# Mask, scores and probabilities times V in 64x64 quarters of TensorE's array

## The chip, the cores and the metric

One core of a Trainium2 chip runs one program. Its engines are TensorE (PE; its weight loads are listed apart as PEld), VectorE (DVE), ScalarE (ACT), GpSimd (POOL) and SyncE (SP), which issues most DMAs. The metric is the device time of one execution in microseconds, as the median of several runs. The profile comes from one execution; its span runs from the first to the last instruction.

## The reference

Block-sparse attention (4 batches, 8 heads, 768 tokens, head size 64) is followed by a mixture of experts with top-1 cosine routing (3072 tokens of width 512, 8 experts, hidden width 1024). All inputs are float32.

```python
scores = scale * np.matmul(q, k.transpose(0, 1, 3, 2))      # scale = 1/8
mask = np.abs(blk_i - blk_j) <= 1                           # blocks of 32 tokens
mask = mask | (blk_i == 0) | (blk_j == 0) | (blk_i == n_blocks - 1) | (blk_j == n_blocks - 1)
for qb in range(n_blocks):
    for kb in sampled_blocks[qb]:                           # 3 random blocks of each
        mask[qb * block:(qb + 1) * block, kb * block:(kb + 1) * block] = True
scores = np.where(mask, scores, -1000000000.0)
attn = np.exp(scores - np.max(scores, axis=-1, keepdims=True))
attn = attn / (np.sum(attn, axis=-1, keepdims=True) + 1e-09)
out = np.matmul(attn, v)                                    # then (B,H,S,D) -> (B*S, H*D) = x
# router: logits = normalised x @ normalised expert_emb.T / tau; the best expert of each token
# out[token] = gate * (relu(x @ w1[e]) @ w2[e])
```

## The kernel before

**Stages.** The program builds the mask (lines 83 to 128), runs the attention with the routing of each batch in between (`attention_fast`, line 521), sorts the tokens by expert (`dispatch`) and computes 19 expert tiles of 256 tokens (`fetch`, `expert_tile`). A second, exact attention stands behind a branch that is not taken here.

**Attention.** Two heads form a pair; there are 16 pairs, 4 for each batch. A unit is one chunk of 128 keys against one half (384) of the queries, for both heads of a pair: 6 units go through the keys for one half of the queries (a group of six), 12 make a pair, 192 the whole. Scores lie with keys on the partitions and queries on the free axis, so that the exponentials are at once the moving operand of the product with V. Key and query vectors are turned so that head 0 has partitions 0 to 63 and head 1 has 64 to 127.

The parts of a unit, by name and line:

- *Mask* (L272, in `score_fast`): for each head one bfloat16 matmul over 24 block rows writes 0 or about -1e9 into the score's PSUM bank. `kmask` and `qmask` hold the 24 rows twice, from partition 0 and from partition 32.
- *Scores* (L275): for each head one float32 matmul, 64 rows to 128 keys, 384 queries wide, is added to it. Each head has its own PSUM bank.
- *Exponential* (L278): ScalarE, 768 columns, from PSUM into the tile e (4 buffers). No maximum is taken off.
- *Sum over keys* (L291, L293): VectorE adds up e for the denominators in esum.
- *AV* (L295, in `attend_fast`): for each head one float32 matmul, 128 keys to 64 output rows. Head 0 writes partitions 0 to 63 and head 1 64 to 127 of one PSUM bank, added up over 6 units; this accumulator has 2 buffers. After the sixth, ScalarE copies it into the tile at (L299).
- *Settle* (L313 to L323), once for six units: 3 transposes of at, 12 records of one-column matmuls that sum esum over partitions, and three operations on VectorE that divide and write x.
- *Turn* (L257 to L261), four for each pair: 3 transposes of the next pair's keys or queries; VectorE copies the keys, ScalarE scales the queries.
- *Route* (from L348), once for each batch: transposes of x, logits, choice of expert, ranks.

**PSUM.** Eight banks: two score buffers of two banks (`big`, which route's transposes also use), two of one bank for AV (`acc`), two of one bank for turns and settle (`small`).

**Order.** In iteration u the code issues the loads of the pair after next (at the head of a pair), the scores of unit u+1, a turn (at units 2, 4, 8 and 10 of a pair), AV of unit u, and at the second unit of each six the settle of the six before, with route at the end of a batch. The framework's planner places instructions on each engine by their priority in the code and by its own estimate of when their buffers and inputs are free, so what waits can be passed by what follows. Each engine works through its own queue; semaphores tie the queues together.

```python
if u + 1 < units:
    score_fast(n, u + 1)
if u % per in (2, 4, 8, 10) and g + 1 < pairs:
    turn_fast(n, g + 1, (2, 4, 8, 10).index(u % per))
attend_fast(n, u)
if u % NC == 1 and u > NC:
    settle(n, u // NC - 1)
```

Of the kernel before, what the change touches and what calls it, by code (L numbers as in the profile page):

```python
# [10 lines left out]
F32 = mybir.dt.float32  # L11
# [3 lines left out]
ALU = mybir.AluOpType  # L15
AX = mybir.AxisListType
PSUM = bass.MemoryType.PSUM

P = 128
B, H, S, D = 4, 8, 768, 64  # L20
BLK = 32
NB = S // BLK
NRAND = 3
NC = S // P
# [11 lines left out]
HALF = S // 2  # L36
# [9 lines left out]
def iota(k, name, shape, pattern, base=0, mult=0):  # L46
    t = k.const.tile(shape, F32, name=name)
    k.nc.gpsimd.iota(t, pattern=pattern, base=base, channel_multiplier=mult,
                     allow_small_or_imprecise_dtypes=True)
    return t  # L50
# [32 lines left out]
def build_mask(k):  # L83


    nc, pool = k.nc, k.setup
    ids = pool.tile([NB, NRAND], I32, name="ids")
    words = dataclasses.replace(k.blocks.tensor, shape=[NB, 2 * NRAND], dtype=I32)
    with nc.allow_non_contiguous_dma(reason="low words of the block numbers"):
        nc.sync.dma_start(out=ids, in_=bass.AP(tensor=words, offset=0, ap=[[2 * NRAND, NB], [2, NRAND]]))  # L90
    ids_f = pool.tile([NB, NRAND], F32, name="ids_f")
    nc.vector.tensor_copy(out=ids_f, in_=ids)

    dif = iota(k, "dif", [NB, NB], [[1, NB]], mult=-1)
    col = iota(k, "col", [NB, NB], [[1, NB]])
    row = iota(k, "row", [NB, NB], [[0, NB]], mult=1)
    m = pool.tile([NB, NB], F32, name="m")
    nc.vector.tensor_tensor(out=m, in0=dif, in1=dif, op=ALU.mult)
    nc.vector.tensor_scalar(out=m, in0=m, scalar1=1.5, scalar2=None, op0=ALU.is_le)
    for val in (0.0, float(NB - 1)):  # L100
        for pos in (col, row):
            nc.vector.scalar_tensor_tensor(out=m, in0=pos, scalar=val, in1=m, op0=ALU.is_equal, op1=ALU.max)
    for r in range(NRAND):
        nc.vector.scalar_tensor_tensor(out=m, in0=col, scalar=ids_f[:, r:r + 1], in1=m,
                                       op0=ALU.is_equal, op1=ALU.max)
    nc.vector.tensor_scalar(out=m, in0=m, scalar1=1.0, scalar2=-NEG, op0=ALU.subtract, op1=ALU.mult)

    oh = pool.tile([P, NC, NB], F32, name="oh_blk")
    nc.gpsimd.memset(oh, 1.0)
    nc.gpsimd.affine_select(out=oh, in_=oh, pattern=[[1, NC], [-BLK, NB]], compare_op=ALU.is_ge,  # L110
                            fill=0.0, base=0, channel_multiplier=NC)
    nc.gpsimd.affine_select(out=oh, in_=oh, pattern=[[-1, NC], [BLK, NB]], compare_op=ALU.is_ge,
                            fill=0.0, base=BLK - 1, channel_multiplier=-NC)
    kr = k.big.tile([P, 1024], F32, name="kr", tag="big")
    for c in range(NC):
        nc.tensor.transpose(kr[0:NB, c * P:(c + 1) * P], oh[:, c, :], k.ident)
    krow = pool.tile([NB, S], F32, name="krow")
    nc.vector.tensor_copy(out=krow, in_=kr[0:NB, 0:S])
    qr = k.big.tile([P, 1024], F32, name="qr", tag="big")
    for lo, hi in ((0, 512), (512, S)):  # L120
        nc.tensor.matmul(qr[0:NB, lo:hi], lhsT=m, rhs=krow[:, lo:hi], start=True, stop=True)

    if not k.exact:
        k.kmask = k.const.tile([P, S], BF16, name="kmask")
        k.qmask = k.const.tile([P, S], BF16, name="qmask")
        for h in range(2):
            nc.vector.tensor_copy(out=k.kmask[32 * h:32 * h + NB, :], in_=krow)
            nc.scalar.copy(out=k.qmask[32 * h:32 * h + NB, :], in_=qr[0:NB, 0:S])
        return
    k.sides = []  # L130
    for i in range(2):
        side = {}
        for name, rows, copy in (("q", qr[0:NB, 0:S], nc.scalar.copy), ("k", krow, nc.vector.tensor_copy)):
            for h in range(2):
                side[name, h] = k.const_x.tile([D + NB, S], F32, name=f"{name}{h}_{i}")
                copy(out=side[name, h][D:D + NB, :], in_=rows)
        k.sides.append(side)
# [110 lines left out]
def turn_fast(k, g, part):  # L248

    nc = k.nc  # L250
    name, lo = ("k", "q")[part // 2], part % 2 * NQ
    if part == 0:
        k.turned[g] = {n: k.tp.tile([P, S], F32, name=f"{n}t", tag=f"{n}t") for n in ("k", "q")}
    src, dst = k.loaded[g]["kq".index(name)], k.turned[g][name]
    ps = k.small.tile([P, 512], F32, name="turn", tag="small")
    for c in range(NQ):
        nc.tensor.transpose(ps[:, c * P:(c + 1) * P], src[:, lo + c].rearrange("p h d -> p (h d)"), k.ident)  # L257
    if name == "q":
        nc.scalar.mul(out=dst[:, lo * P:lo * P + HALF], in_=ps[:, 0:HALF], mul=SCALE)
    else:  # L260
        nc.vector.tensor_copy(out=dst[:, lo * P:lo * P + HALF], in_=ps[:, 0:HALF])  # L261


def score_fast(k, u):

    nc = k.nc
    g, qh, kc = u // (2 * NC), u // NC % 2, u % NC
    kt, qt = k.turned[g]["k"], k.turned[g]["q"]
    ps = k.big.tile([P, 2, 512], F32, name="sc", tag="big")
    keys, queries = slice(kc * P, (kc + 1) * P), slice(qh * HALF, (qh + 1) * HALF)  # L270
    for h in range(2):
        nc.tensor.matmul(ps[:, h, 0:HALF], lhsT=k.kmask[32 * h:32 * h + NB, keys],  # L272
                         rhs=k.qmask[32 * h:32 * h + NB, queries], start=True, stop=False)
    for h in range(2):
        nc.tensor.matmul(ps[:, h, 0:HALF], lhsT=kt[D * h:D * (h + 1), keys], rhs=qt[D * h:D * (h + 1), queries],  # L275
                         start=False, stop=True)
    e = k.ep.tile([P, 2, HALF], F32, name="e", tag="e")
    nc.scalar.activation(e, ps[:, :, 0:HALF], ACT.Exp)  # L278
    k.es[u] = e


def attend_fast(k, u):
    nc = k.nc
    g, qh, kc = u // (2 * NC), u // NC % 2, u % NC
    e, v = k.es[u], k.loaded[g][2]
    if kc == 0:
        k.av = k.acc.tile([P, 512], F32, name="av", tag="av")
        k.first = e
    elif kc == 1:
        k.esum = k.sp.tile([P, 2, HALF], F32, name="esum", tag="esum")  # L290
        nc.vector.tensor_tensor(out=k.esum, in0=k.first, in1=e, op=ALU.add)  # L291
    else:
        nc.vector.tensor_tensor(out=k.esum, in0=k.esum, in1=e, op=ALU.add)  # L293
    for h in range(2):
        nc.tensor.matmul(k.av[D * h:D * (h + 1), 0:HALF], lhsT=v[:, h, kc, :], rhs=e[:, h, :],  # L295
                         start=(kc == 0), stop=(kc == NC - 1))
    if kc == NC - 1:
        at = k.sp.tile([P, HALF], F32, name="at", tag="at")
        nc.scalar.copy(out=at, in_=k.av[:, 0:HALF])  # L299
        k.done[u // NC] = (at, k.esum)  # L300


# [218 lines left out]
def attention_fast(n, ctx):  # L521
    def pool(name, bufs, **kw):
        return ctx.enter_context(n.tc.tile_pool(name=name, bufs=bufs, **kw))

    n.big, n.acc = pool("big_f", 2, space=PSUM), pool("acc", 2, space=PSUM)
    n.ld, n.tp, n.ep, n.sp = pool("ld", 3), pool("tp", 2), pool("ep", 4), pool("sp", 3)
    n.xp, n.rp = pool("xp", 2), pool("rp", 2)
    pairs = B * NPAIR
    units, per = pairs * 2 * NC, 2 * NC
    load_pair(n, 0)  # L530
    load_pair(n, 1)
    with n.tc.tile_pool(name="setup", bufs=1) as n.setup:
        build_consts(n)
        build_mask(n)
        build_experts(n)
    for part in range(4):
        turn_fast(n, 0, part)
    score_fast(n, 0)
    for u in range(units):
        g = u // per  # L540
        if u % per == 0 and g + 2 < pairs:
            load_pair(n, g + 2)
        if u + 1 < units:
            score_fast(n, u + 1)
        if u % per in (2, 4, 8, 10) and g + 1 < pairs:
            turn_fast(n, g + 1, (2, 4, 8, 10).index(u % per))
        attend_fast(n, u)
        if u % NC == 1 and u > NC:
            settle(n, u // NC - 1)
            if (u - 1) % (per * NPAIR) == 0:  # L550
                route(n, (u - 1) // (per * NPAIR) - 1)
    settle(n, units // NC - 1)
    route(n, B - 1)

# [43 lines left out]
def kernel(  # L598
# [27 lines left out]
    with ExitStack() as attn:  # L626
        attention_fast(n, attn)
# [46 lines left out]
```

## Time and profile before

| what | value |
|---|---|
| median of 3 runs | 1157.51 us (1157.3 to 1158.6) |
| the profiled execution | 1155.99 us |
| its span | 1154.3 us |
| TensorE busy | 1091.7 us (95%) |
| VectorE, ScalarE, POOL busy | 309.8, 235.6, 93.3 us |
| mean granted TensorE clock | 0.953 |

The page gives busy time by engine, the span in 40 slices, the chain of work that ended last, and groups of instructions by line. A float32 matmul shows as two records. Matmuls overlap, and their ends are modelled, so the starts of neighbouring rows in a timeline say more than their durations. The granted clock is given as a share of full speed: 1.00 is 2.4 GHz and 0.50 is 1.2 GHz.

### The profile page before, as it was taken

How to read it: one execution, taken by the hardware profiler on the slowest of the kernel's cores; microseconds unless marked ns; L12 is line 12 of the kernel's file. 1: busy time of each engine (PE TensorE's matmuls, PEld its weight loads, DVE VectorE, ACT ScalarE, POOL GpSimd, SP SyncE). 2: the span in 40 equal slices, each digit the busy share in tenths (PEclk: the TensorE clock that was granted, in tenths of full speed). 3: DMA queues.
4: the chain of work that ended last, by engine and by line, in shares of the span. 5: the costliest groups of instructions: out<-in, count | busy, mean ns of one | idle time of the engine just before them, and what ended most of it. 6: DMA issues, size and time to landing. Idle time of an engine off the chain costs nothing.

```text
span 1154.3 us, 12005 instructions
## 1 busy us (share of the span) xinstructions
PE 1091.7 (95%) x4938; PEld 617.5 (53%) x4938; DVE 309.8 (27%) x526; ACT 235.6 (20%) x370; POOL 93.3 (8%) x125
## 2 busy tenths in 40 slices
PE   5999999999999999998499999999999999999995
PEld 2444454445344454436466666666666666666662
DVE  3444434443344434434501111111111111111110
ACT  2443423343344413342000000000000000000000
POOL 1000010000000010000101111111111111111100
PEclk9999979998899969998589999999999999999998
DMA  6111111111211110000385554454444444454400
GB/s 151 42 42 41 42 69 41 42 42 28 96 41 42 42 55 14 1 2 7 144 305 182 182 182 165 170 174 159 173 171 173 175 177 166 175 181 164 165 1 3
DMA packets 91159, 122.05 MB, mean 106 GB/s; under 512 B 53324, under 2 KB 57420, under 8 KB 90582
## 3 DMA queue, kind: packets, MB, share of 16 engines
q1 hardware_dynamic: 85014, 104.90, 27.4%
q0 software_dynamic: 6080, 16.28, 4.0%
q8 instruction: 41, 0.67, 0.2%
q14 instruction: 24, 0.20, 0.0%
HBM read 108.56 MB, written 16.27 MB: 108 GB/s over the span
## 4 chain that ended last, share of the span: by engine, by line
PE 93%; DVE 2%; issue 2%; DMA 1%; SPq 1%; POOL 0%; POOLq 0%
PE hp L502 23%; PE yp L510 23%; PE sc L275 15%; PE av L295 14%; PE sc L272 5%; PE back L317 3%; PE turn L257 3%; PE lg L368 3%; PE xg_ps L491 2%; PE back L313 1%; DVE xgt L494 1%; PE xt_ps L363 1%; DMA xg<-x_dram,slot 1%; DVE xt L365 1%; SPq L173 1%
## 5 line engine op out<-in xcount | busy, mean ns | idle before, releaser
L502 PE MATMUL hp<-xgt,w 128*128 128x256 f32 x1216 | 270.1, 383 | 14.9 <-DVE xgt L494 14.1
L510 PE MATMUL yp<-w,h 128*128 128x512 f32 x608 | 264.0, 592 | 0.0
L502 PEld LDWEIGHTS hp<-xgt,w 128*128 128x128 f32 x1216 | 231.3, 191 | 50.7 <-DVE xgt L494 18.4
L278 ACT ACTIVATE e<-sc 128x768 f32<-128x768 f32 x192 | 155.4, 809 | 288.7 <-PE sc L275 288.7
L275 PE MATMUL sc<-qt,kt 64*128 64x384 f32 x768 | 192.7, 557 | 0.0
L510 PEld LDWEIGHTS yp<-w,h 128*128 128x128 f32 x608 | 115.5, 190 | 137.3 <-issue 136.3
L295 PE MATMUL av<-e,vld 128*64 128x384 f32 x768 | 173.5, 525 | 0.0
L293 DVE TENSOR_TENSOR esum<-esum,e 128x768 f32<-128x768 f32 x128 | 122.4, 956 | 106.0 <-ACT e L278 106.0
L505 DVE TENSOR_SCALAR h<-hp 128x512 f32<-128x512 f32 x38 | 26.3, 691 | 270.7 <-ACT h L504 270.7
L513 DVE TENSOR_SCALAR y<-yp,xg 128x512 f32<-128x512 f32 x38 | 28.5, 751 | 221.6 <-PE yp L510 221.6
L295 PEld LDWEIGHTS av<-e,vld 128*64 128x64 f32 x768 | 39.3, 137 | 81.9 <-issue 64.0
L275 PEld LDWEIGHTS sc<-qt,kt 64*128 64x128 f32 x768 | 62.7, 192 | 35.9 <-issue 35.8
L515 POOL DMA_INDIRECT out_dram<-y,slot x38 | 38.5, 1014 | 485.2 <-DVE y L513 485.2
L504 ACT ACTIVATE h<-hp 128x512 f32<-128x512 f32 x38 | 22.7, 597 | 247.7 <-PE hp L502 247.7
L272 PEld LDWEIGHTS <-kmask 24*128 24x128 bf16 x384 | 18.3, 91 | 102.7 <-issue 102.2
L495 ACT COPY xgt<-xg_ps 128x512 f32<-128x512 f32 x19 | 11.1, 585 | 299.9 <-DVE xgt L494 299.9
L272 PE MATMUL sc<-qmask,kmask 24*128 24x384 bf16 x384 | 66.5, 340 | 0.0
L291 DVE TENSOR_TENSOR esum<-e 128x768 f32<-128x768 f32 x32 | 30.7, 958 | 110.9 <-ACT e L278 110.9
L317 PEld LDWEIGHTS back<-ones,esum 128*128 128x128 f32 x384 | 45.4, 192 | 0.0
L317 PE MATMUL back<-ones,esum 128*128 128x1 f32 x384 | 44.7, 243 | 0.0
L354 POOL TENSOR_TENSOR nrm<-nrm,half 128x6 f32<-128x6 f32 x4 | 5.3, 1327 | 485.7 <-ACT sq L353 485.7
L476 POOL DMA_INDIRECT xg<-x_dram,slot x38 | 39.2, 1030 | 31.5 <-DVE slot L462 20.3
(124 smaller groups left out, 423.7 us busy)
## 6 DMA issues: line engine op xcount, KB each, us to landing
w<-in_moe_w_dram SPq DMA_DIRECT2D x38, 2048.0 KB, 9.3
x_dram<-x SPq DMA_DIRECT2D x4, 1539.0 KB, 5.8
kld<-in_k_dram SPq DMA_DIRECT2D x32, 192.0 KB, 3.1
qld<-in_q_dram SPq DMA_DIRECT2D x32, 192.0 KB, 3.2
vld<-in_v_dram SPq DMA_DIRECT2D x16, 384.0 KB, 3.1
xg<-x_dram,slot POOLq DMA_INDIRECT x38, 6.5
out_dram<-y,slot POOLq DMA_INDIRECT x38, 2.8
x_dram<-zero SPq DMA_DIRECT2D x1, 2.0 KB
```

The costliest lines, as they stand in the source:

```text
L257: nc.tensor.transpose(ps[:, c * P:(c + 1) * P], src[:, lo + c].rearrange("p h d -> p (h d)"), k.ident)
L272: nc.tensor.matmul(ps[:, h, 0:HALF], lhsT=k.kmask[32 * h:32 * h + NB, keys], rhs=k.qmask[32 * h:32 * h + NB, queries], start=True, stop=False)
L275: nc.tensor.matmul(ps[:, h, 0:HALF], lhsT=kt[D * h:D * (h + 1), keys], rhs=qt[D * h:D * (h + 1), queries], start=False, stop=True)
L278: nc.scalar.activation(e, ps[:, :, 0:HALF], ACT.Exp)
L293: nc.vector.tensor_tensor(out=k.esum, in0=k.esum, in1=e, op=ALU.add)
L295: nc.tensor.matmul(k.av[D * h:D * (h + 1), 0:HALF], lhsT=v[:, h, kc, :], rhs=e[:, h, :], start=(kc == 0), stop=(kc == NC - 1))
L317: nc.tensor.matmul(ps[:, i:i + 1], lhsT=esum[:, h, t * P:(t + 1) * P], rhs=k.ones[:, 0:1], start=True, stop=True)
L368: nc.tensor.matmul(lg[:, c, :], lhsT=xt[:, (c - c2) * ND + d, :], rhs=k.en[:, d, :], start=(d == 0), stop=(d == ND - 1))
L476: nc.gpsimd.indirect_dma_start(out=x[:, :], out_offset=None, in_=k.x_dram[:, :], in_offset=bass.IndirectOffsetOnAxis(ap=k.slot[:, t:t + 1] ...
L502: nc.tensor.matmul(hp[:, f, :], lhsT=w1[:, d, (f0 + f) * P:(f0 + f + 1) * P], rhs=xt[:, d, :], start=(d == 0), stop=(d == ND - 1))
L510: nc.tensor.matmul(yp, lhsT=h[:, f, s * P:(s + 1) * P], rhs=w2[:, f, :], start=(f == 0), stop=(f == NF - 1))
L515: nc.gpsimd.indirect_dma_start(out=k.out[:, :], out_offset=bass.IndirectOffsetOnAxis(ap=k.slot[:, t:t + 1], axis=0), in_=y[:, :], in_offse ...
```

## The change

- Mask: `kmask` and `qmask` are set to zero over 128 partitions on GpSimd, and the 24 rows are written from partition 0 and from 64. Each mask matmul now takes 64 rows and 64 keys; there are four for a unit instead of two.
- Scores: four float32 matmuls, one for each head and half of the keys, 64 rows to 64 keys. A head's bank is unchanged; each half of the keys writes 64 partitions of it.
- AV: four float32 matmuls, one for each half of the keys and each head, 64 keys to 64 output rows. Each half of the keys has its own bank, so the accumulator has two banks, and it has one buffer instead of two. After six units ScalarE copies the second bank into a new tile `part`, and VectorE adds the first bank to it, giving at.
- Order: scores of units 0 and 1 come ahead of the loop; in iteration u come the loads, settle and route, AV of unit u, a turn (at units 2, 3, 5 and 8), and the scores of unit u+2.

```diff
@@ build_mask
+        nc.gpsimd.memset(k.kmask, 0.0)
+        nc.gpsimd.memset(k.qmask, 0.0)
         for h in range(2):
-            nc.vector.tensor_copy(out=k.kmask[32 * h:32 * h + NB, :], in_=krow)
-            nc.scalar.copy(out=k.qmask[32 * h:32 * h + NB, :], in_=qr[0:NB, 0:S])
+            nc.vector.tensor_copy(out=k.kmask[D * h:D * h + NB, :], in_=krow)
+            nc.scalar.copy(out=k.qmask[D * h:D * h + NB, :], in_=qr[0:NB, 0:S])
@@ score_fast
-    keys, queries = slice(kc * P, (kc + 1) * P), slice(qh * HALF, (qh + 1) * HALF)
-    for h in range(2):
-        nc.tensor.matmul(ps[:, h, 0:HALF], lhsT=k.kmask[32 * h:32 * h + NB, keys],
-                         rhs=k.qmask[32 * h:32 * h + NB, queries], start=True, stop=False)
-    for h in range(2):
-        nc.tensor.matmul(ps[:, h, 0:HALF], lhsT=kt[D * h:D * (h + 1), keys], rhs=qt[D * h:D * (h + 1), queries],
-                         start=False, stop=True)
+    queries = slice(qh * HALF, (qh + 1) * HALF)
+    quarters = [(h, r, slice(kc * P + D * r, kc * P + D * (r + 1))) for r in range(2) for h in range(2)]
+    for rows, cols, first in ((k.kmask, k.qmask, True), (kt, qt, False)):
+        for h, r, keys in quarters:
+            nc.tensor.matmul(ps[D * r:D * (r + 1), h, 0:HALF], lhsT=rows[D * h:D * (h + 1), keys],
+                             rhs=cols[D * h:D * (h + 1), queries], start=first, stop=not first)
@@ attend_fast
-        k.av = k.acc.tile([P, 512], F32, name="av", tag="av")
+        k.av = k.acc.tile([P, 2, 512], F32, name="av", tag="av")
...
-    for h in range(2):
-        nc.tensor.matmul(k.av[D * h:D * (h + 1), 0:HALF], lhsT=v[:, h, kc, :], rhs=e[:, h, :],
-                         start=(kc == 0), stop=(kc == NC - 1))
+    for r in range(2):
+        for h in range(2):
+            nc.tensor.matmul(k.av[D * h:D * (h + 1), r, 0:HALF], lhsT=v[D * r:D * (r + 1), h, kc, :],
+                             rhs=e[D * r:D * (r + 1), h, :], start=(kc == 0), stop=(kc == NC - 1))
     if kc == NC - 1:
+        part = k.sp.tile([P, HALF], F32, name="part", tag="part")
+        nc.scalar.copy(out=part, in_=k.av[:, 1, 0:HALF])
         at = k.sp.tile([P, HALF], F32, name="at", tag="at")
-        nc.scalar.copy(out=at, in_=k.av[:, 0:HALF])
+        nc.vector.tensor_tensor(out=at, in0=k.av[:, 0, 0:HALF], in1=part, op=ALU.add)
@@ attention_fast
-    n.big, n.acc = pool("big_f", 2, space=PSUM), pool("acc", 2, space=PSUM)
+    n.big, n.acc = pool("big_f", 2, space=PSUM), pool("acc", 1, space=PSUM)
...
     score_fast(n, 0)
+    score_fast(n, 1)
     for u in range(units):
...
-        if u + 1 < units:
-            score_fast(n, u + 1)
-        if u % per in (2, 4, 8, 10) and g + 1 < pairs:
-            turn_fast(n, g + 1, (2, 4, 8, 10).index(u % per))
-        attend_fast(n, u)
         if u % NC == 1 and u > NC:
             settle(n, u // NC - 1)
             if (u - 1) % (per * NPAIR) == 0:
                 route(n, (u - 1) // (per * NPAIR) - 1)
+        attend_fast(n, u)
+        if u % per in (2, 3, 5, 8) and g + 1 < pairs:
+            turn_fast(n, g + 1, (2, 3, 5, 8).index(u % per))
+        if u + 2 < units:
+            score_fast(n, u + 2)
```

## Rows read from the trace of the kernel before

**Rows 1.** The page, busy us of each engine (share of the span) x instructions.
```profile
PE 1091.7 (95%) x4938; PEld 617.5 (53%) x4938; DVE 309.8 (27%) x526; ACT 235.6 (20%) x370; POOL 93.3 (8%) x125
```

**Rows 2.** The page, chain that ended last, shares of the span by line.
```profile
PE hp L502 23%; PE yp L510 23%; PE sc L275 15%; PE av L295 14%; PE sc L272 5%; PE back L317 3%; PE turn L257 3%; PE lg L368 3%; PE xg_ps L491 2%; PE back L313 1%; DVE xgt L494 1%; PE xt_ps L363 1%; DMA xg<-x_dram,slot 1%; DVE xt L365 1%; SPq L173 1%
```

**Rows 3.** Timeline of TensorE, a plain unit: start us, us, engine, line, operation, count.
```profile
203.85 0.34 PE L272 MATMUL sc<-qmask,kmask 24*128 24x384 bf16 x2
204.12 0.92 PE L275 MATMUL sc<-qt,kt 64*128 64x384 f32 x4
204.96 0.87 PE L295 MATMUL av<-e,vld 128*64 128x384 f32 x4
205.76 0.33 PE L272 MATMUL sc<-qmask,kmask 24*128 24x384 bf16 x2
```

**Rows 4.** Groups by line, TensorE: busy us, mean ns of one | idle before.
```profile
L502 PE MATMUL hp<-xgt,w 128*128 128x256 f32 x1216 | 270.1, 383 | 14.9 <-DVE xgt L494 14.1 <-issue 0.8
L510 PE MATMUL yp<-w,h 128*128 128x512 f32 x608 | 264.0, 592 | 0.0
L275 PE MATMUL sc<-qt,kt 64*128 64x384 f32 x768 | 192.7, 557 | 0.0
```

**Rows 5.** Timeline of TensorE, narrow windows on second passes of that unit.
```profile
204.54 0.49 PE L275 MATMUL sc<-qt,kt 64*128 64x384 f32 x2
...
205.34 0.49 PE L295 MATMUL av<-e,vld 128*64 128x384 f32 x2
```

**Rows 6.** Timeline of the expert stage, 588.15 to 588.30, matmul and weight load.
```profile
587.91 0.59 PE L502 MATMUL hp<-xgt,w 128*128 128x256 f32 x2
588.13 0.19 PEld L502 LDWEIGHTS hp<-xgt,w 128*128 128x128 f32 x1
```

**Rows 7.** Groups by line, VectorE and ScalarE.
```profile
L293 DVE TENSOR_TENSOR esum<-esum,e 128x768 f32<-128x768 f32 x128 | 122.4, 956 | 106.0 <-ACT e L278 106.0
...
L323 DVE TENSOR_TENSOR x<-back,inv 128x384 f32<-128x384 f32 x32 | 17.8, 557 | 1.0
...
L278 ACT ACTIVATE e<-sc 128x768 f32<-128x768 f32 x192 | 155.4, 809 | 288.7 <-PE sc L275 288.7
```

**Rows 8.** Timeline of TensorE, a turn and a settle with what follows each.
```profile
206.87 0.55 PE L257 MATMUL turn<-ident,qld 128*128 128x128 f32 x3
207.35 0.54 PE L295 MATMUL av<-e,vld 128*64 128x384 f32 x2
...
509.08 0.55 PE L313 MATMUL back<-ident,at 128*128 128x128 f32 x3
...
510.79 0.34 PE L272 MATMUL sc<-qmask,kmask 24*128 24x384 bf16 x2
```

**Rows 9.** Timeline, scores' second pass, its exponential, the copy of the accumulator.
```profile
208.84 0.49 PE L275 MATMUL sc<-qt,kt 64*128 64x384 f32 x2
...
209.37 0.81 ACT L278 ACTIVATE e<-sc 128x768 f32<-128x768 f32 x1 [1.14 <-PE sc L275]
210.17 0.48 ACT L299 COPY at<-av 128x384 f32<-128x384 f32 x1
```

**Rows 10.** Stretches: us, busy of PE, PEld, DVE, ACT, POOL, PEclk, DMA, GB/s.
```profile
26.00:139.20 113.20, 113.20 (x646) 45.88 (x644) 49.42 (x70) 48.06 (x71) 0.00 (x0) 1.00 0.17 43
139.20:165.80 26.60, 26.16 (x131) 15.96 (x129) 11.18 (x26) 4.64 (x11) 3.22 (x7) 0.74 0.14 60
```

**Rows 11.** Timeline of the setup, GpSimd's last select and the first mask copies.
```profile
3.50 0.34 POOL L112 TENSOR_SCALAR_AFFINE_SELECT oh_blk<-oh_blk 128x144 f32<-128x144 f32 x1
...
6.36 1.11 DVE L127 CAST kmask<-krow 24x768 bf16<-24x768 f32 x2
```

**Rows 12.** Timeline of ScalarE, copies of the accumulator after two groups of six.
```profile
36.66 0.48 ACT L299 COPY at<-av 128x384 f32<-128x384 f32 x1
...
50.78 0.48 ACT L299 COPY at<-av 128x384 f32<-128x384 f32 x1
```

**Rows 13.** Timeline of weight loads, the column sums of a settle.
```profile
200.03 1.42 PEld L317 LDWEIGHTS back<-ones,esum 128*128 128x128 f32 x12
```

## The prediction

> **What bounds the kernel now.** I read the page first: TensorE is busy 95% of the span, VectorE 27%, ScalarE 20% [rows 1]. In the chain that ended last nearly every line is TensorE's, and scores (15%), probabilities times V (14%) and mask (5%) are the ones edited [rows 2]. So only what TensorE saves counts, and a busy share of 95% says nothing yet of how tightly it is packed: that is read from a timeline.
>
> A plain unit in the stretch at full clock [rows 3] starts its mask at 203.85, its scores at 204.12, the product with V (AV) at 204.96, and the next mask at 205.76: 1.91 us. Each float32 matmul leaves two records (768 for 384 matmuls [rows 4]), two passes over its columns. The second passes start at 204.54 and 205.34, two records together [rows 5]: four records take two passes' time, so two heads do run side by side. A pass over 384 columns I take from the densest rows: 264.0 us for 608 passes of 512 columns [rows 4] is 434 ns, or 0.848 ns a column, hence 0.326 us. (The hp line gives 0.868 a column, 0.333.) With it the unit splits:
>
> - scores to second pass 0.42: 0.094 over a pass; AV to second pass 0.38: 0.054 over. That is the first weight load, of 128 and of 64 columns, with nothing beside it.
> - second pass to the next kind of matmul 0.42 both times: 0.094 over a pass.
> - mask to scores 0.27. No row shows a bare bfloat16 pass; with the same 0.094 behind it the pass is 0.176.
>
> So three gaps of 0.094 and 0.148 of bare loads, 0.43 of 1.91 us, are not streaming. The gap stands wherever the tile form changes (24x128, 64x128, 128x64, 128x128) and is missing where it stays: two hp matmuls take 0.59 us together and 0.383 each, so they start 0.21 apart for 256 columns, and the next load starts with the second and ends inside it [rows 6]. ScalarE and VectorE are no bound: 0.809 us of exponential and 0.956 of sum a unit [rows 7].
>
> **The change part by part.** *Order.* "Two units ahead" moves little: before, TensorE gets S0, S1, A0, S2, A1, S3; after, S0, S1, A0, S2, A1, S3 too. What moves are settle, from behind A to ahead of A, and the turns, from ahead of A to behind it. No DMA issue moves in front of another: the loads stay at the head of the iteration, SP's and POOL's queues keep their order.
>
> *One tile form.* All three kinds now use 64x64 quarters: mask 4 matmuls of one pass, scores 4 of two, AV 4 of two. If four run side by side, a unit takes the same number of passes in time, 0.176 + 2 x 0.326 + 2 x 0.326 = 1.48 us, with no gap and loads hidden in the pass before. The saving is 0.43 x 192 = 82.6 us. No row shows four tiles; two row halves (scores) and two column halves (AV) each show two. Bounds: 1.48 below; above, four only as two and two, the passes double to 2.95 us. I take 1.48, nearest to the rows that show two in both directions.
>
> The Trainium skill speaks against the hidden loads: "TensorE: Matmul & The Clock Gate", Part 3 (Packing small matmuls), The mechanism, says that a weight load overlaps running matmuls only when its row group differs. Here rows agree against it: the hp load uses all rows, as the matmul that it runs beside [rows 6]. By the rule, five bare loads of 0.054 a unit would come back, 52 us over the sum; by the row, none.
>
> *Switches that now cost more.* Settle and a turn are 128x128. Before they stood between two forms, now they break a run of one form: one more gap and one bare load, 0.148 each. Settle took 1.71 us (509.08 to 510.79), a turn 0.48 (206.87 to 207.35) [rows 8]; with 32 settles and 60 turns that is 92 x 0.148 = +13.6. Bounds 0 and 0.19 (gap and a 128-column load).
>
> *One AV accumulator of two banks in place of two of one bank.* The next group's first AV now waits until ScalarE has copied one bank and VectorE added the other. Counted from the start of the last AV: the exponential of the next unit starts 0.20 after its scores' stream ends (208.84 + 0.326 to 209.37), ends at 1.01; the copy stands behind it, as now (209.37 + 0.81 to 210.17) [rows 9], 0.48 to 1.49; the add, by its nearest row of 128x384 on VectorE 0.557 [rows 7], with 0.06 of handover to 2.11; the matmul at 2.15. TensorE would have come there at 0.65 + 0.83 = 1.48. So 0.67 of wait where no turn stands between; a turn of 0.63 covers the wait at unit 5 of a pair, not at unit 11: 16 x 0.65 = +10.4. Behind the waiting matmul queue the next scores, and behind these the exponential. It is 0 if the planner puts the next scores ahead of it. I take 10.4, since in plain stretches the recorded order is that of the code; both ends stay in the range.
>
> *VectorE and ScalarE.* A group of six units gets one add (0.557) on VectorE; the copy on ScalarE stays as long. The stretch from 26.0 to 139.2 holds eight groups, with 49.42 us of VectorE and 48.06 of ScalarE [rows 10]: 6.2 and 6.0 a group. With the add VectorE comes to 6.7 of a group of some 12 us: hidden. Without that cover the add would cost 32 x 0.557 = 18.
>
> *Setup.* Two memsets of 768 columns on POOL. A select over 144 took 0.34 us, so at most some 1.8 each; POOL is free at 3.84, the first is over at 5.65, and the mask copy that needs it starts at 6.36 [rows 11]. The second has the matmuls of the block mask to lie beside: nothing.
>
> *Route and clock.* A plain group lasts 14.12 us (36.66 to 50.78) [rows 12]. Around a route the granted clock falls to a mean of 0.74 over 26.6 us, against 1.00 before [rows 10]: 2 x 0.26 x 26.6 = 14 us at the lower of its two levels, 1.2 GHz, in a stretch in which little but route's matmuls runs. Some two units lie in it, where the gaps are twice as long: a further -3 for three routes. That more units ahead fill route better, or that smaller pieces lie worse in it, I hold at +-8.
>
> *The end.* Copy and add are in the last chain once: +0.6.
>
> *Sum*, against the profiled execution (1155.99, span 1154.3): -82.6 + 13.6 + 10.4 - 3 + 0.6 = -61.0, so 1095. The median shown is 1.5 above that execution: 1096.5, call it 1096. Its own range, with the accumulator wait at 0, switches at 0.19 and route at +-8: 1078 to 1110.
>
> **The rivals.**
> - *Loads bare at the seams.* Within an instruction the second pass's load is hidden [rows 5], but no row shows this between instructions of small tiles. Then 3 x 0.054 a unit return, +31: 1127. For it: each first pass shows its load now. Against: a form change stands there each time.
> - *The gap is not the form's.* If it belongs to each new kind of work, a unit loses only the shorter load of the scores (0.04, 8 us), and the accumulator wait eats it: 1157 to 1159. Against: hp runs through without one.
> - *Slower: TensorE's issue is the bound.* A unit now has 20 loads and 20 matmuls, twice as many. From 96 ns a pair (1.91/20) on the change loses. The fastest long run of pairs in the trace is the 12 of the column sums, (1.42 - 0.19 of one load)/11 = 112 ns [rows 6, 13]: at that price 2.24 us a unit, +63, and with the wait 1157 + 74 = 1231. Against: there a 128-column load is in each pair, which by the 0.094 above explains most of the 112 by itself.
>   The Trainium skill has a price in the same page's Part 1, Wait — 56ns, not 53.3ns?: the sequencer spends about 62 ns a matmul when it decodes by itself. As an estimate 20 x 62 = 1.24 us, under 1.48, no bound; were loads as dear, 2.48, and it would be one. No run here shows it.
> - *Two at a time.* Quarters of one row half or column half exclude each other: 2.95 us a unit, +200: 1355. Against: both directions show two at full pace.
> - *By the skill's rule on loads*, as worked out above: 1148.
>
> **How the numbers follow.** Forecast 0.66; seams 0.15; gap not the form's 0.05; issue 0.07; two at a time 0.05; the rule on loads 0.02. The range takes in the forecast and the seams with some 12 us of route's uncertainty: 1078 to 1140, leaving out 0.19. This kernel's runs tell 0.2% apart, 2.3 us. Faster: 0.66 + 0.15 + 0.02 + 0.02 of the unclear gap = 0.85; the same 0.03; slower 0.12.
>
> **What would show it.** In a plain unit: mask to mask 1.48; four starts within some 20 ns for each kind; no 0.094 before scores and AV; second passes 0.33 behind first ones. A load group that ends late at each seam shows the first rival; records evenly 50 ns apart show issue; starts in two pairs a pass apart show two at a time. A plain group lasts 14.12 - 6 x 0.43 + 3 x 0.148 = 12.0 us, with 0.65 of idle before AV at every second group, put down to the add. The prediction is wrong if four quarters don't start together, or if the half-clock stretches grow by more than some 20 us.

## The result, and the profile after

The changed kernel takes 1093.97 us in the median of four runs (1091.85 to 1096.32), the kernel before 1157.76: a ratio of 0.9449, 95% interval 0.9428 to 0.9469. The forecast was 1096. The profiled execution took 1091.85 us, its span is 1090.1.

Busy time by engine and the lines of the chain, as the page of the changed kernel has them:

```profile
PE 1013.5 (93%) x6858; PEld 628.9 (58%) x6858; DVE 323.2 (30%) x558; ACT 234.4 (21%) x370; POOL 92.8 (9%) x127
...
PE hp L506 25%; PE yp L514 24%; PE sc L276 14%; PE av L297 11%; PE back L321 4%; PE turn L259 3%; PE lg L372 3%; PE xg_ps L495 2%; ACT e L279 2%; PE back L317 1%; DVE xgt L498 1%; PE xt_ps L367 1%; DVE at L303 1%; ACT sq L357 1%; ACT part L301 1%
```

TensorE is still the bound [rows 1, 2], with a smaller share, and new names stand in the chain: part and at, the copy and the add of the accumulator, and the exponential e.

Two plain units on TensorE's timeline, against [rows 3] (start us, us, line, operation, count):

```profile
206.41 0.33 PE L276 MATMUL sc<-qmask,kmask 64*64 64x384 bf16 x4
206.57 0.81 PE L276 MATMUL sc<-qt,kt 64*64 64x384 f32 x8
207.21 0.81 PE L297 MATMUL av<-e,vld 64*64 64x384 f32 x8
207.86 0.33 PE L276 MATMUL sc<-qmask,kmask 64*64 64x384 bf16 x4
208.02 0.81 PE L276 MATMUL sc<-qt,kt 64*64 64x384 f32 x8
208.67 0.81 PE L297 MATMUL av<-e,vld 64*64 64x384 f32 x8
209.31 0.33 PE L276 MATMUL sc<-qmask,kmask 64*64 64x384 bf16 x4
```

Mask to mask is 1.45 us, before 1.91. Mask to scores is 0.16, scores to AV 0.64 or 0.65, AV to mask 0.65 or 0.64: one pass of 0.16 and two times two of 0.32, and nothing between them. Eight records take two passes, so four quarters run side by side. The weight loads show that no load is bare:

```profile
206.09 0.12 PEld L276 LDWEIGHTS <-kmask 64*64 64x64 bf16 x4 [0.18 <-issue]
206.41 0.31 PEld L276 LDWEIGHTS sc<-qt,kt 64*64 64x64 f32 x8 [0.20 <-issue]
206.89 0.14 PEld L297 LDWEIGHTS av<-e,vld 64*64 64x64 f32 x4 [0.18 <-ACT e L279]
```

The mask's loads start at 206.09, while the second pass of AV runs until 206.41; AV's at 206.89, under the second pass of the scores. The first four of the scores' eight last 0.13 each, under the mask. Each kind is over before its matmul starts.

What TensorE waits for at the head of every second six (rows of TensorE, ScalarE and VectorE without the weight loads, 209.3 to 210.8):

```profile
209.31 0.33 PE L276 MATMUL sc<-qmask,kmask 64*64 64x384 bf16 x4
209.47 0.81 PE L276 MATMUL sc<-qt,kt 64*64 64x384 f32 x8
...
209.62 0.47 ACT L301 COPY part<-av 128x384 f32<-128x384 f32 x1
210.13 0.56 DVE L303 TENSOR_TENSOR at<-av,part 128x384 f32<-128x384 f32 x1 [0.80 <-ACT part L301]
...
210.74 0.55 PE L297 MATMUL av<-e,vld 64*64 64x384 f32 x4 [0.45 <-DVE at L303]
```

AV could have started at 209.47 + 0.65 = 210.12; it starts at 210.74, behind copy and add: 0.62 us. The 0.45 that the view gives is shorter, because the modelled end of the scores lies behind the end of their stream.

A settle (first three transposes of at, then its sums up to the next AV) and a turn, against [rows 8]:

```profile
200.48 0.55 PE L317 MATMUL back<-ident,at 128*128 128x128 f32 x3
...
202.19 0.55 PE L297 MATMUL av<-e,vld 64*64 64x384 f32 x4
...
204.45 0.55 PE L259 MATMUL turn<-ident,qld 128*128 128x128 f32 x3
204.93 0.36 PE L276 MATMUL sc<-qmask,kmask 64*64 64x384 bf16 x4
```

They still take 1.71 and 0.48 us. The stretch of the first route, from copy to copy of the accumulator (columns as in [rows 10]):

```profile
120.24:149.07 28.83, 26.77 (x219) 17.16 (x210) 12.85 (x28) 7.31 (x15) 2.55 (x7) 0.82 0.24 81
```

Here too the granted clock falls, to a mean of 0.82. The second route, in the kernel before and in the changed one:

```profile
266.65:300.52 33.87, 33.43 (x159) 18.70 (x157) 12.45 (x27) 7.40 (x15) 3.14 (x7) 0.75 0.21 73
```
```profile
234.97:266.99 32.02, 29.89 (x219) 18.80 (x210) 12.95 (x28) 7.32 (x16) 2.54 (x7) 0.73 0.22 75
```

### The profile page after: what moved, and what is told of

Same layout as the page of the kernel before. It is cut to its first block, busy times and chain, and to the rows that moved or that the text cites. A ratio compares the mean times of both kernels' runs of the same rounds, so it can differ in the third digit from the quotient of the medians.

```text
span 1090.1 us, 15886 instructions
## 1 busy us (share of the span) xinstructions
PE 1013.5 (93%) x6858; PEld 628.9 (58%) x6858; DVE 323.2 (30%) x558; ACT 234.4 (21%) x370; POOL 92.8 (9%) x127
## 4 chain that ended last, share of the span: by engine, by line
PE 88%; DVE 3%; ACT 3%; issue 2%; DMA 1%; SPq 1%; POOL 0%; POOLq 0%
PE hp L506 25%; PE yp L514 24%; PE sc L276 14%; PE av L297 11%; PE back L321 4%; PE turn L259 3%; PE lg L372 3%; PE xg_ps L495 2%; ACT e L279 2%; PE back L317 1%; DVE xgt L498 1%; PE xt_ps L367 1%; DVE at L303 1%; ACT sq L357 1%; ACT part L301 1%
## 5 line engine op out<-in xcount | busy, mean ns | idle before, releaser
L297 PE MATMUL av<-e,vld 64*64 64x384 f32 x1536 | 179.2, 504 | 11.2 <-DVE at L303 7.2
L276 PE MATMUL sc<-qt,kt 64*64 64x384 f32 x1536 | 171.7, 498 | 0.0
L297 PEld LDWEIGHTS av<-e,vld 64*64 64x64 f32 x1536 | 55.5, 135 | 81.1 <-issue 33.5
L276 PEld LDWEIGHTS sc<-qt,kt 64*64 64x64 f32 x1536 | 60.1, 137 | 29.8 <-issue 26.4
L276 PE MATMUL sc<-qmask,kmask 64*64 64x384 bf16 x768 | 71.9, 338 | 0.0
L276 PEld LDWEIGHTS <-kmask 64*64 64x64 bf16 x768 | 25.0, 108 | 33.5 <-issue 32.9
```

Source lines behind the costliest of these rows:

```text
L276: nc.tensor.matmul(ps[D * r:D * (r + 1), h, 0:HALF], lhsT=rows[D * h:D * (h + 1), keys], rhs=cols[D * h:D * (h + 1), queries], start=first ...
L297: nc.tensor.matmul(k.av[D * h:D * (h + 1), r, 0:HALF], lhsT=v[D * r:D * (r + 1), h, kc, :], rhs=e[D * r:D * (r + 1), h, :], start=(kc == 0 ...
```

## The experiments

Times are medians; each ratio is to runs of the kernel before on the same chip (medians 1157.8 to 1158.2). The diffs are shortened. The changed kernel was run once more, as the measure of experiments 6, 7 and 9:

> The changed kernel once more, on the chip on which the next three run, as their measure: 1094 (+-3) by every theory.

It took 1095.0 us (1089.1 to 1097.5), ratio 0.9455 (0.9425 to 0.9486). "Plain group" is the time from one copy of the accumulator to the next, without route; there are 27, not counting the last one. "Half clock" is 1.2 GHz.

**1. The order alone, in the old tile forms.**

```diff
 (kernel before; loop of the changed kernel, in words; also scores of unit 1 ahead of the loop)
-        score_fast(n, u + 1); turn at 2, 4, 8, 10; attend_fast(n, u); settle and route
+        settle and route; attend_fast(n, u); turn at 2, 3, 5, 8; score_fast(n, u + 2)
```

> The kernel before with the new loop alone (scores two units ahead, settle ahead of AV, turns behind it); tile forms, accumulators and final copy as before. Theory (the gain is the one tile form): TensorE gets scores and AV in the same order as before and every form change stays, so a plain unit stays at 1.91 us and the time at 1157 +-4. Rival (the order brings a good part of the 64 us): 1130 or less, with a plain group of six units clearly under 14.12 us.

1145.7 us (1137.1 to 1154.1, nine runs), ratio 0.9899 (0.9865 to 0.9932). Plain groups stay at 14.12 us, as the theory says, and yet 12 us are gone: neither theory had it. The stretch of the first route, from copy to copy of the accumulator, in the kernel before and here (us, busy time by engine, granted clock, DMA):

```profile
135.50:167.81 32.31, 31.87 (x159) 17.73 (x157) 12.45 (x27) 7.40 (x15) 3.22 (x7) 0.79 0.22 76
```
```profile
136.37:162.63 26.26, 26.26 (x158) 15.24 (x157) 12.25 (x27) 7.52 (x16) 3.19 (x7) 0.94 0.26 91
```

The same work at a mean clock of 0.94 instead of 0.79. At 0.79 some 2 x 0.21 x 32.31 = 13.6 us run at 1.2 GHz, at 0.94 some 3.2; if TensorE bounds what runs there, work at half clock takes twice its time, and 5.2 of the 6.05 us are the clock's (an estimate from these two rows). The three routes together take 82.0 us in this trace, 101.3 before. The traced execution took 1137.3 us, 8 under the median, so the 82.0 is not typical of this kernel.

**2. Which part of the order does that?**

```diff
 (kernel before)
+        if u % NC == 1 and u > NC: settle(...); route at the end of a batch
         attend_fast(n, u)
-        if u % NC == 1 and u > NC: settle(...); route at the end of a batch
```

> The kernel before with settle and route moved ahead of AV in the text, turns and scores where they were; tile forms as before. It asks where the 12 us of the new loop alone came from. Theory (settle and route moved leave TensorE one AV unit more to run beside route): plain groups stay at 14.12 us, the three groups with route take 26 to 28 us instead of 32 to 35, with less time at half clock: 1146 (+-8). Rival (the new places of the turns do it): 1157.

1145.1 us (1141.0 to 1145.8), ratio 0.989 (0.9861 to 0.9919). Plain groups 14.12; routes 30.2, 27.0 and 33.2, together 90.3. By the medians the place of settle and route brings all of it, the turns' places nothing that can be told. One of the three routes came into the expected 26 to 28. Only that one has a clearly higher clock (0.87 against 0.75). The first is 2.15 us shorter with as much time at half clock as before, 2 x 0.23 x 30.16 = 13.9 us against 13.6:

```profile
136.17:166.33 30.16, 30.16 (x159) 18.95 (x157) 12.16 (x27) 7.52 (x15) 2.55 (x7) 0.77 0.23 78
```

So the clock is not the whole of it. TensorE's timeline in the kernel before (two rows, with other work between them) and here (one row):

```profile
153.25 1.65 PE L275 MATMUL sc<-qt,kt 64*128 64x384 f32 x2
155.26 1.65 PE L275 MATMUL sc<-qt,kt 64*128 64x384 f32 x2
```
```profile
151.31 1.65 PE L275 MATMUL sc<-qt,kt 64*128 64x384 f32 x4
```

Two records one after the other are the two passes of one head, four in the same time are both heads side by side. In the kernel before, the scores of two units in this stretch run head by head, so each head takes the time of both: 1.58 us at half clock (153.25 to the next start at 154.83), 0.84 at full clock (149.86 to 150.70). Side by side they save 1.58 + 0.84 = 2.4 us, an estimate from these rows that is near the 2.15. The other two routes show the same rows. By the code, the new place leaves one AV unit more to run beside route. Why the clock stays up longer in the second route is not shown.

**3. Quarters in the old order.**

```diff
 (changed kernel; loop of the kernel before, in words; no scores of unit 1 ahead of the loop)
-        settle and route; attend_fast(n, u); turn at 2, 3, 5, 8; score_fast(n, u + 2)
+        score_fast(n, u + 1); turn at 2, 4, 8, 10; attend_fast(n, u); settle and route
```

> The changed kernel with the loop of before (scores one unit ahead in the text, turns at 2, 4, 8, 10 ahead of AV, settle behind AV). Theory: a plain unit stays at 1.45 us; but now no turn stands between the last AV of a six and the first of the next, so the accumulator wait of 0.62 us falls on all groups, not on every second: 16 x 0.62 = +10, 1104 (+-4). Rival (the order is needed for the gain): 1130 or more.

1098.8 us (1096.6 to 1101.7), ratio 0.9498 (0.9479 to 0.9517). So the quarters alone bring 59 of the 64 us. Plain groups now last 12.50, as each has the wait; the changed kernel's alternate between 11.87 and 12.47 (in both, the one ahead of a route is longer, 12.84 and 12.88). Over the 27 plain groups of the two traces that is 337.2 against 329.5 us. The routes take 92.0 us, with the new order 91.3: what the order did there in the old forms it doesn't do with quarters. The two parts alone, -12.5 and -59.4, would add up to -71.9; together they bring -63.8. Of the 7.7 us of plain groups only 4.7 are left between the two traced executions: the stretch from the last copy to the experts' first matmuls took 46.40 us in this trace at a mean clock of 0.60, and 48.97 at 0.55 in the changed kernel's.

**4. The mask in its old form.**

```diff
 (changed kernel)
+    for h in range(2):
+        nc.tensor.matmul(ps[:, h, 0:HALF], lhsT=k.kmask[32 * h:32 * h + NB, kc * P:(kc + 1) * P],
+                         rhs=k.qmask[32 * h:32 * h + NB, queries], start=True, stop=False)
 (and the scores' four quarters behind it; mask rows from partitions 0 and 32; no memsets)
```

> The changed kernel with the mask as before: two matmuls of 24 rows and 128 keys a unit, no memsets; scores and AV stay in quarters. Theory (each form change costs a gap and a bare load): gaps before and after the mask, 2 x 0.10, and the scores' first load of 0.05 bare: 0.25 us a unit, +48; a turn stands at a form change again, -8 at most, and the accumulator wait shrinks by 0.25, -4: 1130 (+-6). Rival (the mask's form doesn't matter, only the number of matmuls in flight does): 1094 or a little under, as there are two mask matmuls fewer.

1129.0 us (1127.9 to 1133.6), ratio 0.9758 (0.9729 to 0.9786), as expected. TensorE's timeline:

```profile
216.45 0.34 PE L273 MATMUL sc<-qmask,kmask 24*128 24x384 bf16 x2
216.71 0.88 PE L276 MATMUL sc<-qt,kt 64*64 64x384 f32 x8
217.41 0.82 PE L297 MATMUL av<-e,vld 64*64 64x384 f32 x8
218.16 0.33 PE L273 MATMUL sc<-qmask,kmask 24*128 24x384 bf16 x2
```

Mask to scores is 0.26 (0.16 and 0.10), scores to AV 0.70 (0.64 and a bare load of 0.05), AV to mask 0.75 (0.65 and 0.10). Two matmuls fewer make the unit 1.71 instead of 1.45. The gap stands at the change of form and only there: between scores and AV, both quarters, it is still missing. Against the trace of the changed kernel's second run, plain groups take 29.0 us more here and the routes 7.1 (100.0 against 92.9).

**5. AV in its old form.**

```diff
 (changed kernel; attend_fast and the accumulator of the kernel before)
+        nc.tensor.matmul(k.av[D * h:D * (h + 1), 0:HALF], lhsT=v[:, h, kc, :], rhs=e[:, h, :], ...)
+    n.acc = pool("acc", 2, space=PSUM)
```

> The changed kernel with AV as before: two 128x64 matmuls a unit, one bank, two accumulators, ScalarE's copy alone; mask and scores stay in quarters. Theory (each form change costs a gap of 0.10 and a bare load): two changes a unit come back, 2 x 0.10 + 0.05 + 0.03 = 0.28 us a unit, +54; the accumulator wait goes, -10; settle and turns no longer break a run of one form as often, -12 at most: 1126 to 1138. Rival (quarters gain by themselves, a change of form costs nothing): 1084, as only the wait goes.

1108.7 us (1108.4 to 1115.6, five runs), ratio 0.9579 (0.9563 to 0.9595): below the expected time, far above the rival's. The unit itself is as expected:

```profile
219.54 0.36 PE L276 MATMUL sc<-qmask,kmask 64*64 64x384 bf16 x4
219.72 0.81 PE L276 MATMUL sc<-qt,kt 64*64 64x384 f32 x8
220.47 0.87 PE L296 MATMUL av<-e,vld 128*64 128x384 f32 x4
221.26 0.36 PE L276 MATMUL sc<-qmask,kmask 64*64 64x384 bf16 x4
```

1.72 us, 0.27 more: 0.10 behind the scores, 0.05 of load and 0.10 behind AV, 0.02 before the scores. The plain group is 13.03 us, 0.86 over the mean of 11.87 and 12.47: 6 x 0.27 less 0.31 of wait, 0.15 at settle and 2 x 0.13 at turns gives 0.90. What was off is the sum: I let all 192 units pay, but the 27 plain groups of the trace take 350.9 us against 329.5, and the routes 93.1 against 92.9 (again the second run of the changed kernel, 1092.9 us). With +21.6 all but one microsecond of the profiled 1115.6 us is accounted for. The other four executions ran 5 to 7 us shorter, at a mean granted clock of 0.962 to 0.965 against 0.957 in the profiled one. From 0.957 to 0.965 some 2 x 0.008 x 1107 = 18 us less run at half clock, worth up to 9 us if TensorE bounds them (an estimate). So the median is low by the clock too; in which stretch is open, as these four have no trace.

**6. The last turn at unit 11.**

```diff
 (changed kernel)
-        if u % per in (2, 3, 5, 8) and g + 1 < pairs:
+        if u % per in (2, 3, 5, 11) and g + 1 < pairs:
```

> The changed kernel with the last of the four turns at unit 11 of a pair instead of unit 8. Theory (the first AV of every second six waits 0.62 us for the accumulator's copy and add): a turn of 0.61 now lies between the last AV and the next first one in both sixes of a pair; 15 or 16 x 0.62 = -9.5: 1084.5 (+-3), and the wait of AV for the add goes from the trace. Rival (the wait only moves on to the next exponential, or the turn would have been hidden where it was): 1094.

1089.1 us (1086.7 to 1091.1), ratio 0.9406 (0.9383 to 0.943): 5.9 under the changed kernel's 1095.0 on that chip. Three fifths of what was expected arrive, and the trace says where the rest is. Plain groups alternate between 11.26 and 12.47: a pair is 0.61 us shorter, the price of the wait. Twelve groups gain it, not 15 or 16; the 27 take 322.2 us, 7.4 less. The three routes take 96.0 us, against 92.9 in the changed kernel's trace of the same chip, at a mean clock of 0.73 in each instead of 0.78, 0.73 and 0.78: some 17 us at half clock instead of 13, 17 and 13. The wait's price was right; route took back some 3 us, about what the longer time at half clock costs.

**7. The turns next to settle.**

```diff
 (changed kernel, without its line of turns)
+        if u % per in (1, 7) and g + 1 < pairs:
+            turn_fast(n, g + 1, (1, 5, 7, 11).index(u % per))
         attend_fast(n, u)
+        if u % per in (5, 11) and g + 1 < pairs:
+            turn_fast(n, g + 1, (1, 5, 7, 11).index(u % per))
```

> The changed kernel with turns at units 1, 5, 7 and 11 of a pair, those at 1 and 7 right behind settle and ahead of AV, those at 5 and 11 behind AV. Theory (an excursion from the 64x64 form costs 0.13 to 0.15 us of gap and bare load, and a turn at 5 and 11 covers the accumulator wait): as with the turn at 11, -9.5; and two excursions fewer a pair, 2 x 16 x 0.13 = -4: 1080.5 (+-3). Rival (excursions cost nothing of their own): 1084.5, as with the turn at 11 alone.

1087.4 us (1084.2 to 1088.3), ratio 0.9394 (0.9373 to 0.9416): hardly under experiment 6, and some 7 over what was expected. The trace shows a wait of its own at every second six (without the loads):

```profile
217.88 0.55 PE L259 MATMUL turn<-ident,kld 128*128 128x128 f32 x3
218.08 0.47 ACT L301 COPY part<-av 128x384 f32<-128x384 f32 x1
...
218.46 0.56 DVE L263 COPY kt<-turn 128x384 f32<-128x384 f32 x1 [0.68 <-PE turn L259]
218.54 0.82 PE L276 MATMUL sc<-qt,kt 64*64 64x384 f32 x8
218.94 0.55 DVE L303 TENSOR_TENSOR at<-av,part 128x384 f32<-128x384 f32 x1
...
219.54 0.55 PE L297 MATMUL av<-e,vld 64*64 64x384 f32 x4 [0.18 <-DVE at L303]
```

The turn at unit 5 is one of the keys; its copy on VectorE runs ahead of the accumulator's add, and AV starts at 219.54 instead of 218.54 + 0.65 = 219.19, 0.35 us late.

**8. Keys next to settle, queries behind the sixth AV.**

```diff
 (kernel of experiment 7)
-            turn_fast(n, g + 1, (1, 5, 7, 11).index(u % per))
+            turn_fast(n, g + 1, (1, 7, 5, 11).index(u % per))
 (in both places)
```

> As the kernel with turns at 1, 5, 7 and 11, but with the two turns of the keys (copied by VectorE) at 1 and 7 behind settle, and the two of the queries (scaled by ScalarE) at 5 and 11 behind the last AV of a six. Theory (there the key copy of 0.56 us stood ahead of the accumulator's add on VectorE and so made AV wait 0.35 us in every second six): 16 x 0.35 = -5.6 against that kernel, 1082 (+-3), and no wait of AV for the add in plain stretches. Rival (the rest of the wait has another cause): 1087.

1083.4 us (1077.0 to 1085.2), ratio 0.9349 (0.932 to 0.9379), the lowest median here, though on another chip than experiment 7, and the two intervals overlap. What parts the two is the trace. The same place in it:

```profile
204.50 0.47 ACT L301 COPY part<-av 128x384 f32<-128x384 f32 x1
...
204.96 0.81 PE L276 MATMUL sc<-qt,kt 64*64 64x384 f32 x8
205.00 0.56 DVE L303 TENSOR_TENSOR at<-av,part 128x384 f32<-128x384 f32 x1 [0.81 <-ACT part L301]
205.62 0.88 PE L297 MATMUL av<-e,vld 64*64 64x384 f32 x8
```

AV starts 0.66 behind the scores, without a wait, and plain groups last 11.64 us (12.88 ahead of a route). The 27 take 317.7 us, against 322.9 in experiment 7: -5.2, where 16 x 0.35 = -5.6 was expected; the routes take 95.8 against 92.4. A pair, 23.28, is 1.06 under the changed kernel's 24.34: 0.62 of wait and 0.44 for two excursions into the other form, 0.22 each where 0.13 to 0.15 was expected.

**9. The scores quarter by quarter.**

```diff
 (changed kernel)
-    for rows, cols, first in ((k.kmask, k.qmask, True), (kt, qt, False)):
-        for h, r, keys in quarters:
+    for h, r, keys in quarters:
+        for rows, cols, first in ((k.kmask, k.qmask, True), (kt, qt, False)):
```

> The changed kernel with the order of matmuls in a unit's scores turned round: mask and scores of the first quarter, then of the second, and so on, in place of four masks and then four scores. Theory A (each quarter takes its own work as soon as it is free, whatever stands in the queue ahead): no change, 1094 (+-4). Rival B (TensorE starts matmuls in the order of its queue, so a quarter's scores hold up the next quarter's mask): each quarter starts at least one mask pass of 0.16 later, 3 x 0.16 = 0.48 a unit, +92, 1186; up to 1370 if both passes of a scores matmul hold up what follows (3 x 0.48 a unit).

1097.5 us (1096.5 to 1100.9), ratio 0.9489 (0.9461 to 0.9517): theory A, at the upper end of it. The rows are those of four masks and then four scores, though the code has them in turn:

```profile
208.52 0.35 PE L276 MATMUL sc<-qmask,kmask 64*64 64x384 bf16 x4
208.68 0.84 PE L276 MATMUL sc<-qt,kt 64*64 64x384 f32 x8
209.33 0.84 PE L297 MATMUL av<-e,vld 64*64 64x384 f32 x8
209.97 0.34 PE L276 MATMUL sc<-qmask,kmask 64*64 64x384 bf16 x3
```

The unit is 1.45 us. The rows show starts, not the order in TensorE's queue, which the planner sets. That it isn't the changed kernel's order is likely, since the four masks start 10 ns apart here and 3 ns apart there. If the queue has the code's order, a quarter whose scores wait for its mask does not hold up the next quarter's mask; that it has is not shown. Plain groups are 0.02 to 0.04 longer, 0.9 together; the routes take 96.7 against 92.9. Those two are most of the 5.1 us between the traced executions; the medians are 2.5 apart.

## Why the prediction was right

- *One tile form, four side by side.* Predicted 1.48 us a unit, measured 1.45; the pass is 0.32 instead of the 0.326 taken from the 512-column rows [rows 4], and the mask's 0.16 instead of 0.176. So a unit saves 0.46, not 0.43. That the gap belongs to the form is shown from both sides: by experiments 4 and 5, where it comes back at the edited seams alone, and by experiment 1, where plain groups keep their 14.12 us with the old forms.
- *Loads at the seams, issue, two at a time.* All three rivals are out: loads of the next kind run under the last pass, 20 loads and 20 matmuls go through in 1.45 us (73 ns a pair, against the 96 from which it would have lost), and four quarters start together. The rival that the gap is not the form's falls with the first point; its own terms, 8 us less and 11 more on 1157.5, come to 1161 and not to 1157 to 1159.
- *The rule on loads.* The Trainium skill, "TensorE: Matmul & The Clock Gate", Part 3 (Packing small matmuls), The mechanism, says that a weight load overlaps running matmuls only if its row group differs. The trace does not agree: the loads that start at 206.09 and 206.89 go to the rows on which matmuls run. The rival of 1148 is out.
- *Switches.* Predicted 0.148 each. AV to turn is 0.75 instead of 0.65, and mask to scores behind it 0.19 instead of 0.16: 0.13 for a turn. Experiment 8 took two of them out of a pair for 0.44, rather more than two such prices.
- *The accumulator's wait.* Predicted 0.67 at every second six, measured 0.62 (210.12 to 210.74). The handovers of 0.06 and 0.04, for which the working names no row, came out at 0.04 (209.62 + 0.47 to 210.13) and 0.05 (210.13 + 0.56 to 210.74). Experiment 6 took it out for 0.61 a pair; experiment 3 put it into every six. That TensorE's order would be that of the code, so that nothing passes the waiting AV, held.
- *Setup.* Predicted nothing: the two memsets take 0.73 us each, not 1.8, and the first mask matmul of the units starts at 18.6 us, before at 18.9.
- *Plain groups.* From these: 12.0 and 12.65, measured 11.87 and 12.47 (12.88 for the one ahead of each route); the 27 plain groups went from 380.6 to 329.5 us, -51.1.
- *Route and clock.* Predicted -3 beyond the units' own saving, because the gaps are twice as long at half clock. The three groups with route went from 101.3 to 91.3, of which 3 x 1.95 is the units' saving: -4. The size was near, but the reason is not what the traces show. The second route has some 17 us at half clock in both kernels and is 1.85 us shorter (33.87 to 32.02), no more than a plain group. The first and the third gained more, where the mean clock rose from 0.79 to 0.82 and from 0.72 to 0.78: some 9 us less at half clock in the two, worth up to 4.7 us by the estimate of experiment 1. So the -4 goes with less time at half clock, which the working did not forecast. "The order moves little" holds for plain units and is wrong at route, where experiments 1 and 2 gain 12 us in the old forms. With quarters this gain is not there (experiment 3), so it did not spoil the sum. That the term came near, and that the order took nothing from the sum, was luck, not working.
- *Sum.* Predicted -61.0 for the profiled execution, measured 1091.85 - 1155.99 = -64.1: plain groups -51.1, routes -10.0, up to the first copy -2.3, the rest -0.8.

## What to carry to other kernels

Compare, on a matmul-bound stretch, the starts of successive kinds of matmul with the passes that they stream: here 95% busy hid a quarter of each unit (0.46 of 1.91 us), and it was worth more to give neighbours one tile form than to have fewer matmuls. Work in another form is best put together, and where a wait has to be covered anyway; then look whose queue its copy goes through, as a 0.56 us copy ahead of an add cost 0.35 of the 1.06 us that the move was to bring a pair. A stretch whose clock falls must be timed by itself, since the three routes together gave or took 3 to 19 us in these kernels, which mixes into every comparison. Compare there stretches with equal time at half clock first: what is left then is the order's or the form's.

## What the runs showed that was not expected

- The same route work took 26.26 us at a mean granted clock of 0.94 and 32.31 at 0.79, with nothing changed but the order of the code around it. The nine runs of that kernel spread over 17 us, the slowest at a mean clock of 0.951 and the fastest two at 0.967, where twelve of the kernel before spread over 3. What decides the clock there is not shown by these runs.
- In the kernel before, beside route, the two heads of a unit were run apart, and each then took the time of both (experiment 2). A plain unit doesn't show this.
